# Spreading attention weights over the partitions: SBUF to SBUF transfers in place of matmuls and copies, and the last store from the ACT queue

## The chip, the cores and the metric
The kernel runs on one core of a Trainium2 chip. The core has a matrix engine (PE, with its weight loads shown as PEld), a vector engine (DVE), a scalar engine (ACT), a general engine (POOL) and a queue engine (SP); SP, ACT and POOL can issue DMA transfers. The metric is the device time of one execution in microseconds (us). The kernel before takes 203.83 us, the median of three runs (202.96 to 204.58).

## The reference
A transformer layer with a local, dilated attention and a gated MLP, 2048 tokens of width 512, in bf16. Cut to what matters:

```python
# S = 2048, D = 512, H = 32 heads of Dh = 16, W = 8 window places, dil = 2, F = 1376
q, k, v = split(layernorm(x) @ wqkv)                # each (H, S, Dh)
idx = pos[:, None] - arange(W)[None, :] * dil       # s, s-2, ..., s-14
logits = einsum("hsd,hswd->hsw", q, k[:, idx]) * Dh ** -0.5   # masked where idx < 0
attn = softmax(logits, axis=-1)                     # over the 8 window places
o = einsum("hsw,hswd->hsd", attn, v[:, idx])
h = x + o @ wo
h2 = h + (relu(layernorm(h) @ W_gate) * (layernorm(h) @ W_up)) @ W_down
```

## The kernel before
The tokens are worked in four chunks of 512 (`tk` 0 to 3). Within a chunk the steps are: layer norm, transposition of the rows (by PE, or for some chunks by a DMA transpose from SP, L472), the q, k and v projections (L524, copied out by ACT, L532), attention, the output projection (L711) with residual (L722, or L720 on ACT for chunk 0), a second layer norm, gate and up projections (L749), their product on DVE (L769), the down projection (L786), the residual (L797) and the store (L801).

Attention works in a layout in which each of the 128 partitions holds one dimension of a head and the free axis holds tokens. The channels are permuted so that a tile `t` (0 to 3) holds four of the 16 dimensions of each of the 32 heads. The parts that the change touches, with the keys the code gives the steps:

- `pr` (L571, DVE): q times shifted k for half of the window places (`hf` 0 or 1) and two tiles; an instruction of 128 x 4096, four per chunk.
- `sc` (L577, PE): sums the products over the head dimension; the score tile of one half holds 32 heads x 4 window places on its 128 partitions.
- `ex` (L593, ACT): the exponential, into an `ex` tile of 128 x 512. In chunk 0 a short mask step `mk` (L596) follows on DVE.
- `den` (L610, PE), `dl` and `dr` (L613, L616, ACT): the sum over the window and its reciprocal. In chunks 1 to 3 (`EARLY`) the weights are multiplied by the reciprocal at once (`am`, L625, DVE); in chunk 0 this is done at the end (`om`, L666).
- `bc` (L638, PE) and `be` (L644, ACT): the weights of one window place stand on 32 partitions, one for each head, but are needed on 128, four for each head. For each half, four matmuls with the 0/1 matrix `spread` (32 rows of contraction, at four row positions of PE) write four banks, and four ACT copies bring them to a tile of 128 x 8 x 512 called `ab`, eight copies per chunk.
- `mu` (L659, DVE): `ab` times shifted v, 128 x 4096, one for each tile `t`.
- `ta` (L691, POOL): in chunks 0 to 2 the first addition of the sum over the window is a DMA that accumulates one half of the `mu` result onto the other, 512 KB. Then `tr2` (128 x 1024) and `tr1` (128 x 512) on DVE (L662, L685), and in chunk 0 `om`.

The results of `pr`, of `mu` and the tile `ab` come from one pool of five tiles of 128 x 8 x 512, named `big`.

The order of the work is not left to the queues. Every step is added to a planner with an engine, an assumed length and an entry of the list `RANK`: the n-th entry is the place of the n-th added step. Each engine gets its steps in increasing order of that place, and it executes them strictly in this order; an instruction waits at the head of its engine's queue until its inputs and its buffer are ready. The planner's lengths decide which buffer a step gets and how the engines' instructions interleave in the program, not the order within one engine.

SP issues, in its order: the loads at the start, the DMA transposes and the output stores. The kernel's last chunk stores its last 128 rows in two halves (columns 0 to 255 as part 3, 256 to 511 as part 4).

Of the kernel before, what the change touches and what calls it, by code (L numbers as in the profile page):

```python
# [8 lines left out]
P = 128  # L9
BF16 = mybir.dt.bfloat16  # L10
F32 = mybir.dt.float32
I32 = mybir.dt.int32
ACT = mybir.ActivationFunctionType
# [6 lines left out]
    26, 31, 32, 17, 20, 22, 23, 25, 29, 34, 35, 28, 33, 37, 39, 41, 45, 48, 21, 27,  # L20
    30, 36, 38, 42, 44, 46, 63, 74, 40, 56, 68, 49, 51, 54, 43, 60, 72, 53, 66, 65,
    77, 70, 83, 75, 80, 90, 92, 87, 114, 102, 110, 85, 105, 93, 104, 115, 125, 129, 78, 88,
    95, 99, 103, 183, 193, 202, 132, 143, 150, 156, 152, 106, 109, 116, 123, 119, 168, 181, 216, 220,
    224, 180, 188, 217, 223, 231, 187, 196, 226, 229, 234, 162, 172, 201, 205, 207, 237, 240, 239, 245,
    247, 251, 242, 248, 243, 246, 252, 256, 259, 263, 250, 254, 265, 266, 272, 278, 269, 276, 285, 275,
    283, 273, 280, 286, 318, 322, 292, 301, 304, 314, 313, 324, 341, 311, 325, 298, 303, 334, 338, 326,
    330, 346, 354, 360, 337, 355, 317, 353, 347, 358, 370, 329, 352, 340, 348, 332, 345, 294, 350, 356,
    361, 374, 343, 365, 372, 381, 351, 362, 413, 357, 368, 367, 386, 418, 400, 425, 460, 464, 417, 427,
    457, 467, 376, 434, 446, 466, 410, 429, 437, 668, 55, 61, 52, 57, 50, 58, 47, 59, 62, 64,
    67, 84, 73, 82, 86, 71, 81, 69, 79, 89, 166, 175, 122, 136, 111, 130, 137, 190, 91, 101,  # L30
    127, 173, 149, 179, 94, 96, 163, 213, 158, 170, 98, 107, 108, 167, 208, 197, 249, 257, 244, 235,
    255, 260, 264, 268, 274, 296, 279, 302, 309, 305, 310, 307, 287, 295, 290, 293, 300, 319, 328, 364,
    369, 315, 320, 359, 363, 335, 342, 380, 382, 327, 336, 373, 375, 389, 395, 387, 392, 396, 402, 393,
    399, 398, 401, 397, 403, 405, 409, 404, 407, 411, 412, 416, 419, 420, 423, 421, 428, 422, 426, 431,
    474, 482, 441, 443, 458, 463, 453, 468, 483, 438, 448, 436, 452, 442, 451, 450, 454, 456, 488, 492,
    479, 498, 455, 487, 491, 500, 507, 461, 493, 445, 459, 481, 485, 471, 475, 496, 511, 539, 524, 533,
    520, 535, 526, 530, 541, 514, 540, 484, 502, 543, 544, 556, 581, 589, 538, 552, 559, 562, 549, 554,
    584, 587, 529, 547, 560, 564, 113, 120, 100, 124, 76, 117, 97, 112, 128, 133, 140, 144, 142, 146,
    164, 145, 154, 148, 157, 161, 209, 230, 174, 186, 198, 200, 195, 215, 182, 184, 199, 228, 189, 211,
    169, 177, 178, 194, 232, 241, 271, 281, 185, 191, 261, 253, 284, 297, 289, 282, 308, 312, 321, 331,  # L40
    339, 344, 378, 366, 377, 371, 379, 383, 385, 394, 388, 391, 390, 430, 439, 470, 490, 424, 432, 473,
    476, 440, 447, 486, 489, 406, 415, 465, 477, 501, 518, 497, 504, 508, 512, 494, 499, 521, 525, 517,
    519, 516, 522, 503, 505, 527, 528, 532, 546, 534, 537, 536, 548, 531, 542, 579, 597, 566, 594, 585,
    601, 561, 580, 609, 599, 603, 588, 592, 571, 575, 577, 600, 605, 606, 610, 595, 623, 602, 611, 582,
    614, 627, 558, 576, 574, 578, 568, 572, 565, 567, 583, 621, 648, 639, 645, 636, 649, 591, 616, 652,
    624, 635, 628, 633, 640, 655, 663, 665, 667, 632, 654, 661, 711, 650, 656, 707, 710, 644, 657, 659,
    669, 126, 138, 118, 134, 131, 139, 121, 135, 141, 147, 155, 160, 151, 171, 159, 165, 153, 176, 203,
    236, 218, 225, 192, 204, 214, 219, 258, 291, 262, 270, 222, 233, 267, 277, 227, 238, 212, 221, 288,
    316, 206, 210, 306, 299, 323, 333, 384, 349, 408, 414, 433, 435, 444, 462, 449, 506, 510, 509, 513,
    515, 469, 495, 478, 472, 480, 563, 570, 586, 593, 523, 551, 557, 569, 573, 590, 596, 598, 545, 550,  # L50
    553, 555, 615, 622, 604, 607, 612, 619, 608, 613, 626, 629, 618, 620, 630, 631, 617, 625, 634, 637,
    638, 641, 646, 653, 643, 651, 642, 647, 691, 695, 681, 692, 694, 698, 688, 697, 700, 679, 687, 674,
    677, 670, 680, 666, 671, 690, 673, 675, 672, 682, 658, 662, 660, 678, 683, 684, 689, 664, 685, 699,
    702, 676, 693, 705, 701, 706, 704, 709, 686, 703, 708, 713, 715, 716, 718, 696, 714, 719, 720, 722,
    724, 731, 712, 726, 732, 734, 717, 725, 727, 730, 728, 733, 735, 737, 721, 723, 729, 736,
]


class Op:


    __slots__ = ("eng", "dur", "lat", "fn", "deps", "prio", "take", "use", "start", "done", "seq", "key")

    def __init__(self, eng, dur, fn, deps=(), prio=0.0, take=(), use=(), lat=0.0):
        self.eng, self.dur, self.fn, self.lat = eng, dur, fn, lat
# [788 lines left out]
```

## Time and profile before
| | |
|---|---|
| median of three runs | 203.83 us (202.96 to 204.58) |
| span of the profiled execution | 200.7 us |
| PE busy | 193.4 us, 1095 instructions |
| DVE busy | 153.3 us, 239 instructions |
| ACT busy | 121.8 us, 256 instructions |
| POOL busy | 12.7 us |
| mean granted PE clock | 0.999 of full speed |
| DMA | 18.81 MB, 94 GB/s on average |

The profile is of one execution; the device time of that execution is its span and some us around it that the profile does not show (203.83 less 200.7 is 3.1 us, by the median). Times within it count from the first instruction. Matmuls are pipelined and their single durations overlap, so their step from one to the next is read from the chain of waits, not from the mean duration. A line such as L659 is the line of the kernel that issued the instruction. Idle time of an engine is followed by what ended it. In the DVE column of the page the slices from 20 to 100 us stand at 9 tenths or more almost throughout; PE stands there from the second slice to the last but one.

### The profile page before, as it was taken

To read this page: it belongs to the slowest core of one execution; us is meant where nothing else is said; L and a number is where in the kernel's file an instruction comes from. 1 tells how busy PE (TensorE), PEld (TensorE's weight loads), DVE (VectorE), ACT (ScalarE), POOL (GpSimd) and SP (SyncE) were. 2 spreads that over 40 slices of the span, in tenths; PEclk is the share of its full clock that TensorE was granted. 3 is DMA by queue.
4 is the path that set the end of the run, shared out by engine and by line. 5 is a ranking of instruction groups with operands and counts; after the bars stand their busy time and mean duration, and the time that the engine had idled before them with its cause. 6 is when DMAs were issued, how large, how long until landed. Compare 5 with 4: busy or idle time off the path is not lost.

```text
span 200.7 us, 2938 instructions
## 1 busy us (share of the span) xinstructions
PE 193.4 (96%) x1095; PEld 96.2 (48%) x1115; DVE 153.3 (76%) x239; ACT 121.8 (61%) x256; POOL 12.7 (6%) x28
## 2 busy tenths in 40 slices
PE   8999999989999999999999999999999999999992
PEld 8776445445445344444444444444444444444451
DVE  6989998989999999999996868799967412022313
ACT  3576798747899965887436779701566631277400
POOL 4000000410000013100131000000000000000000
PEclk9999999999999999999999999999999999999999
DMA  6989933994000009920399400131010050200103
GB/s 204 322 245 409 388 119 66 170 201 87 3 0 0 3 0 183 195 40 3 57 178 193 124 3 0 29 75 52 3 52 0 0 104 3 78 0 0 52 0 105
DMA packets 17676, 18.81 MB, mean 94 GB/s; under 512 B 8352, under 2 KB 14464, under 8 KB 17664
## 3 DMA queue, kind: packets, MB, share of 16 engines
q1 hardware_dynamic: 15360, 11.57, 18.5%
q0 software_dynamic: 1728, 6.29, 16.6%
q10 hardware_dynamic: 576, 0.79, 1.2%
q8 instruction: 8, 0.13, 0.3%
q14 instruction: 4, 0.03, 0.0%
HBM read 8.42 MB, written 2.10 MB: 52 GB/s over the span
## 4 chain that ended last, share of the span: by engine, by line
PE 67%; DVE 16%; DMA 6%; ACT 5%; issue 2%; SPq 1%; ACTq 0%
PE bank L749 29%; PE bank L524 15%; PE bank L786 14%; DVE big L659 6%; PE bank L711 5%; DMA quad<-row 5%; DVE big L571 3%; DVE gT L769 2%; DMA x_sm<-in_A_x_dram 1%; SPq L472 1%; PE bank L483 1%; DVE x_sm L722 1%; DVE big L662 1%; DVE row L454 1%; PE bank L577 1%
## 5 line engine op out<-in xcount | busy, mean ns | idle before, releaser
L749 PE MATMUL bank<-quad,wu_sb 128*128 128x512 bf16 (+1 forms) x172 | 42.4, 379 | 0.4
L749 PE MATMUL bank<-quad,wg_sb 128*128 128x512 bf16 (+1 forms) x173 | 42.0, 379 | 0.4 <-DMA quad<-row 0.3
L756 ACT ACTIVATE gr<-bank 128x512 bf16<-128x512 f32 (+1 forms) x44 | 25.3, 616 | 24.7 <-PE bank L749 22.9
L786 PE MATMUL bank<-wd_sb,gT 128*128 128x512 bf16 (+2 forms) x183 | 39.8, 366 | 0.2
L753 ACT CAST up_sb<-bank 128x512 bf16<-128x512 f32 (+1 forms) x44 | 25.0, 600 | 21.0 <-PE bank L749 17.3
L571 DVE TENSOR_TENSOR big<-quad,kT 128x4096 bf16<-128x4096 bf16 x16 | 36.2, 2284 | 0.2
L659 DVE TENSOR_TENSOR big<-big,vT 128x4096 bf16<-128x4096 bf16 x16 | 35.9, 2281 | 0.0
L769 DVE TENSOR_TENSOR gT<-gr,up_sb 128x1024 bf16<-128x1024 bf16 (+1 forms) x24 | 15.3, 642 | 24.0 <-ACT up_sb L753 14.4
L524 PE MATMUL bank<-quad,wqk_sb 128*128 128x512 bf16 (+1 forms) x139 | 29.9, 355 | 1.0 <-DMA quad<-row 0.8
L786 PEld LDWEIGHTS <-gT 128*128 128x128 bf16 (+1 forms) x187 | 18.1, 98 | 19.7 <-issue 0.4
L749 PEld LDWEIGHTS <-wg_sb 128*128 128x128 bf16 (+1 forms) x176 | 17.3, 100 | 21.2 <-issue 0.9
L749 PEld LDWEIGHTS <-wu_sb 128*128 128x128 bf16 (+1 forms) x176 | 17.5, 100 | 20.6 <-issue 0.7
L524 PEld LDWEIGHTS <-wqk_sb 128*128 128x128 bf16 x144 | 15.6, 114 | 12.8 <-issue 2.3
L797 DVE TENSOR_TENSOR row<-x_sm,bank 128x512 bf16<-128x512 bf16 (+1 forms) x17 | 10.6, 649 | 10.4 <-PE bank L786 10.4
L644 ACT CAST big<-bank 128x512 bf16<-128x512 f32 x32 | 17.8, 635 | 0.4 <-PE bank L638 0.2
L662 DVE TENSOR_TENSOR big<-big 128x1024 bf16<-128x1024 bf16 (+2 forms) x24 | 16.8, 728 | 0.1
L691 POOL DMA_DIRECT2D big<-big x12 | 10.5, 873 | 88.1 <-DVE big L659 59.9
L524 PE MATMUL bank<-quad,wv_sb 128*128 128x512 bf16 x62 | 15.6, 380 | 0.2
L711 PE MATMUL bank<-wo_sb,quad 128*128 128x512 bf16 x62 | 15.2, 379 | 0.2
L454 DVE TENSOR_SCALAR row<-x_sm,mv,rs 128x512 bf16<-128x512 bf16 x32 | 11.4, 407 | 3.7 <-ACT rs L436 3.1
L532 ACT CAST quad<-bank 128x512 bf16<-128x512 f32 x16 | 9.5, 612 | 4.6 <-PE bank L524 4.6
L499 ACT COPY quad<-bank 128x1024 bf16<-128x1024 bf16 (+1 forms) x9 | 8.0, 929 | 6.0 <-PE bank L483 6.0
(68 smaller groups left out, 147.2 us busy)
## 6 DMA issues: line engine op xcount, KB each, us to landing
big<-big POOLq DMA_DIRECT2D x12, 512.0 KB, 5.6
out_dram<-row SPq DMA_DIRECT2D x15, 128.0 KB, 1.8
x_sm<-in_A_x_dram SPq DMA_DIRECT2D x3, 512.0 KB, 5.5
wu_sb<-in_B_W_up_dram SPq DMA_DIRECT2D x1, 1376.0 KB, 8.6
wg_sb<-in_B_W_gate_dram SPq DMA_DIRECT2D x1, 1376.0 KB, 11.6
wd_sb<-in_B_W_down_dram SPq DMA_DIRECT2D x1, 1280.0 KB, 14.9
wqk_sb<-in_A_wqkv_dram ACTq DMA_DIRECT2D x2, 256.0 KB, 5.0
wqk_sb<-in_A_wqkv_dram SPq DMA_DIRECT2D x2, 256.0 KB, 5.2
```

What stands on the lines that cost most here:

```text
L454: V.tensor_scalar(out=xn.t[:], in0=x, scalar1=mv.t[:, j, 0:1], scalar2=rs.t[:, j:j + 1], op0=ALU.add if residual else ALU.subtract, op1=AL ...
L524: nc.tensor.matmul(mm.t[:, lo:hi], lhsT=wv_sb[:, dt, t:D:NT] if c == 2 else wqk_sb[:, dt, c * D + t:(c + 1) * D:NT], rhs=xnT.t[:, dt, lo:h ...
L571: V.tensor_tensor(out=pb.t[:].rearrange("p (t w) s -> p t w s", t=2), in0=q4, in1=k4, op=ALU.mult)
L644: nc.scalar.copy(out=ab.t[:, w, :], in_=bc.t[:])
L659: V.tensor_tensor(out=mt.t[:], in0=ab.t[:], in1=v8, op=ALU.mult)
L662: V.tensor_tensor(out=mt.t[:, 0:n, :], in0=mt.t[:, 0:n, :], in1=mt.t[:, n:2 * n, :], op=ALU.add)
L711: nc.tensor.matmul(od.t[:], lhsT=OT.t[:, t, j * P:(j + 1) * P], rhs=wo_sb[:, t, :], start=(t == 0), stop=(t == NT - 1 and tk not in RPE))
L749: nc.tensor.matmul(mm.t[:fs, :], lhsT=w_sb[:, dt, ft * P: ft * P + fs], rhs=hnT.t[:, dt, :], start=(dt == 0), stop=(dt == NT - 1))
L753: nc.scalar.copy(out=ub.t[:fs, i, :], in_=um.t[:fs, :])
L756: nc.scalar.activation(out=gr.t[:fs, i, :], in_=gm.t[:fs, :], func=ACT.Relu)
L769: V.tensor_tensor(out=gt.t[:fs, 0:n, :], in0=gr.t[:fs, 0:n, :], in1=ub.t[:fs, 0:n, :], op=ALU.mult)
L786: nc.tensor.matmul(od.t[:, c0:c1], lhsT=gts[ft].t[:fs, ft % 2, j * P:(j + 1) * P], rhs=wd_sb[:fs, ft, c0:c1], start=(ft == 0), stop=(ft == ...
```

## The change
For every chunk and half (`BCD`), the four matmuls and four ACT copies are replaced by four DMA transfers issued from SP, with the step key `bd`. Each reads the 32 partitions of one window place and writes each row to four neighbouring partitions, 128 rows of 1 KB. The tile `ab` gets a pool of its own with one tile, and the pool `big` shrinks from five to four. The store of the very last part (part 4 of chunk 3) is issued from ACT's queue. `RANK` is new throughout, with 706 entries where it had 738. The options `PRE` and `DEN1` are empty, so their branches are never taken. The planner learns of a shared DMA queue (`dq`) and has some lengths changed; these change no instruction.

```diff
-    big_s = slots(5, [P, W, CS], BF16, "big")
+    NAB = 1
+    big_s = slots(5 - NAB, [P, W, CS], BF16, "big")
+    ab_s = slots(NAB, [P, W, CS], BF16, "ab") if NAB else big_s
...
+    BCD = tuple((k, h) for k in range(4) for h in range(2))
...
-        ab, abd = Buf(big_s), []
+        ab, abd = Buf(ab_s), []
         for w0 in range(0, W, BCN):
             hf = w0 // 4
+            if (tk, hf) in BCD:
+                def f_bd(w0=w0, ab=ab, ex=exs[hf]):
+                    for w in range(w0, w0 + 4):
+                        r = w % 4 * HB
+                        nc.sync.dma_start(ab.t[:, w, :], ex.t[r:r + HB, :].unsqueeze(1).to_broadcast([HB, 4, CS]))
+
+                abd.append(add(("bd%d" % hf, tk), "SP", 4 * DMI, f_bd, [exd[hf]], apr + 1, take=[ab],
+                               use=[exs[hf]], lat=0.7, dq=(0.2, 1.54 - 3 * DMI)))
+                continue
...
+            last = tk == NCK - 1 and n == len(parts) - 1
+
+            def f_os(j=j, c0=c0, c1=c1, ob=ob, tk=tk, q=nc.scalar if last else nc.sync):
+                q.dma_start(out_rows[:, tk * BPC + j, c0:c1], ob.t[:, c0:c1])
```

Read entry by entry, the new `RANK` gives these orders (key, then chunk after the point; `xtd` and `htd` are the DMA transposes of the first and second layer norm, `hxn` the normalised rows of the second, `gu` the gate x up products, `o` the residuals of the MLP, `os` the stores). SP before, to chunk 2:

```
xtd0.3 xtd2.3 xtd1.3 xtd3.3 htd0.1 htd1.1 os0.0 os2.0 os1.0 htd1.2 htd3.2 htd0.2 htd2.2
```

SP after, to chunk 2, and its end:

```
bd1.0 bd0.0 xtd1.3 xtd3.3 xtd0.3 xtd2.3 bd1.1 bd0.1 bd0.2 bd1.2 htd1.1 htd0.1 bd0.3 os3.0 bd1.3 os1.0 os0.0 htd3.2
... os2.2 os0.3 os1.2 os0.2 os1.3 os2.3 os3.3
```

DVE before, from the second mask step of chunk 0 to the middle of chunk 1's attention (`xst`, `xag` statistics, `xxn` normalised rows of the first layer norm):

```
mk0.0 xst.3 xag.3 (4) xxn.2 (4) xxn.3 (4) mu3.0 mu0.0 mu1.0 mu2.0 pr0_2.1 tr2_3.0 tr1_3.0 om3.0 pr0_0.1 tr2_0.0 tr2_1.0
tr1_0.0 tr1_1.0 om0.0 tr2_2.0 tr1_2.0 om1.0 om2.0 ... am1.1 pr1_2.2 pr1_0.2 am0.1 pr0_2.3 pr0_0.3 mu1.1 mu0.1 mu3.1 mu2.1
gu0.0 am0.2 gu1.0 pr1_2.3 gu3.0 tr2_1.1 tr1_1.1 tr2_0.1 tr1_0.1 gu2.0 ...
```

DVE after, the same stretch and on to chunk 3's first `mu`:

```
mk0.0 xst.3 (2) xag.3 (3) xxn.2 (4) xxn.3 (3) mu3.0 xxn2.3 mu0.0 mu1.0 mu2.0 tr2_3.0 tr1_3.0 om3.0 pr0_0.1 tr2_0.0 tr1_0.0
om0.0 tr2_1.0 tr1_1.0 pr0_2.1 om1.0 tr2_2.0 tr1_2.0 om2.0 ... am1.1 hxn0.0 hxn1.0 am0.1 pr0_0.2 pr0_2.3 mu1.1 pr0_0.3 mu3.1
mu0.1 gu1.0 tr2_1.1 mu2.1 gu2.0 tr1_1.1 am0.2 pr1_0.3 am1.2 gu0.0 tr2_0.1 gu3.0 tr2_3.1 tr1_0.1 tr1_3.1 gu4.0 tr2_2.1
tr1_2.1 mu0.2 ... hxn1.1 ... mu1.2 o3.0 mu2.2 o2.0 mu3.2 am1.3 am0.3 o1.0 tr2_1.2 tr2_0.2 o0.0 tr1_0.2 tr1_1.2 tr2_2.2
gu0.1 tr1_2.2 gu1.1 tr2_3.2 tr1_3.2 mu3.3
```

PE before, from the end of chunk 0's attention to its first down projection (`htp` transposes, `ga` and `up` the gate and up projections, `dnA` the first 8 and `dnB` the last 3 column tiles of the down projection):

```
wo2.0 sc0.1 sc1.1 mm_q2.3 mm_k2.3 den.1 mm_k3.3 mm_v2.2 htp.0 (4) sc0.2 bc1.1 mm_v2.3 ga0.0 ... up9.0 dnA2.0
```

PE after:

```
wo3.0 sc1.1 mm_v3.2 mm_k1.3 den.1 mm_v2.2 mm_v1.3 sc1.2 mm_k0.3 htp.0 (4) mm_v0.3 up4.0 ... up10.0 dnA0.0
```

and its end is `... dnA2.3 dnB2.3 dnA3.3 dnB3.3`.

## The prediction
> **What bounds the kernel now.** I read the busy times first, then the windows of ten microseconds, then the chain that ended last, then the timeline around the edited lines, and last the DMA issues. Page and windows (busy time, with the number of instructions in brackets; the last three columns are the granted clock, the DMA share and GB/s):
> ```profile
> PE 193.4 (96%) x1095; PEld 96.2 (48%) x1115; DVE 153.3 (76%) x239; ACT 121.8 (61%) x256; POOL 12.7 (6%) x28
> ```
> ```profile
> 0.00:10.00 10.00, 8.51 (x91) 8.01 (x92) 7.63 (x28) 4.10 (x11) 2.20 (x16) 1.00 0.78 264
> ...
> 40.00:50.00 10.00, 9.30 (x43) 4.98 (x45) 9.36 (x12) 5.76 (x12) 0.86 (x1) 1.00 0.76 147
> ...
> 60.00:70.00 10.00, 9.85 (x82) 4.67 (x84) 10.00 (x11) 9.94 (x21) 0.00 (x0) 1.00 0.01 2
> 70.00:80.00 10.00, 9.95 (x63) 4.19 (x57) 10.00 (x5) 6.43 (x13) 2.58 (x3) 1.00 0.45 85
> ...
> 190.00:201.00 11.00, 7.10 (x43) 4.08 (x42) 3.14 (x6) 0.00 (x0) 0.00 (x0) 0.97 0.15 48
> ```
> PE is idle 7.3 us of 200.7, and 5.4 of that lie in the first and the last window. In between it is full, so the time is start + PE's own list + tail, and every us taken off PE's list counts unless a wait takes its place. Right behind PE stands DVE: full from 50 to 100 us. ACT is full only around 55 to 70.
>
> **The matmuls removed.** Lines of the chain (start, length, what):
> ```profile
> 21.70 1.85 PE bank L524 x8
> 23.55 0.33 PE bank L638 x4
> 23.88 1.85 PE bank L524 x8
> ...
> 122.83 4.32 PE bank L749 x20
> ```
> A group of four spreading matmuls holds PE 0.33 us. A normal matmul takes 4.32/20 = 0.216, so eight should take 1.73; beside a spreading group they take 1.85, so the change of form costs up to 0.12 more. Eight groups are removed: 8 x 0.33 = 2.6 to 8 x 0.45 = 3.6 us. I take 0.40 each, 3.2 us, since some groups stand next to score matmuls of the same kind. It all lies on PE's list.
>
> **The ACT copies removed.**
> ```profile
> L644 ACT CAST big<-bank 128x512 bf16<-128x512 f32 x32 | 17.8, 635 | 0.4 <-PE bank L638 0.2
> ...
> L638 PE MATMUL bank<-ex,spread 32*128 32x512 bf16 x32 | 3.2, 384 | 0.0
> ```
> In the chain one copy steps on by 0.49 us, so ACT loses 32 x 0.49 = 15.7 us. ACT is not the path, so this is worth nothing by itself; it hides under PE and DVE. What it can free is waits on ACT: DVE waits 0.47 us for the reciprocal at 44.1, 0.44 for the residual at 53.5, and 0.57 at 31 for a row buffer behind PE. Together 1.5 us of DVE's time, which matters because of what follows.
>
> **The transfers added.** Per chunk eight SyncE DMAs, each 128 rows of 1 KB, from 32 partitions. No such transfer is in the trace. The nearest rows (median us from issue to landing):
> ```profile
> big<-big POOLq DMA_DIRECT2D x12, 512.0 KB, 5.6
> out_dram<-row SPq DMA_DIRECT2D x15, 128.0 KB, 1.8
> ...
> quad<-row SPq DMA_TRANSPOSE x14, 2.5
> ```
> ```profile
> 196.06 2.29 SPq L801 DMA_DIRECT2D out_dram<-row  x5
> ```
> The row store has the same size and the same 1 KB rows: 1.8 us to land, and five issues take 2.29, so 0.46 each. Four issues for one half of the windows: 3 x 0.46 + 1.8 = 3.2 us, which I take because that row is nearest in size, form and queue. The lower end is 3 x 0.39 + 1.6 = 2.8 (the shortest of the store rows), the upper end 5.6 (512 KB in SBUF beside other traffic). The way replaced:
> ```profile
> 28.48 0.40 PE L638 MATMUL bank<-ex,spread 32*128 32x512 bf16 x4
> ...
> 28.96 0.59 ACT L644 CAST big<-bank 128x512 bf16<-128x512 f32 x1
> ...
> 29.55 1.55 ACT L644 CAST big<-bank 128x512 bf16<-128x512 f32 x3
> ...
> 31.77 8.89 DVE L659 TENSOR_TENSOR big<-big,vT 128x4096 bf16<-128x4096 bf16 x4
> ```
> From 28.48 to 31.10 is 2.6 us, so the new way has 0.2 to 3.0 us more latency. Who waits for it is the first mu multiply of a chunk, with all of DVE's list queued behind. Its cover is the DVE work that the new list has between the last ex or am step and that mu, with the steps of this trace (pr and mu 2.2, bn_stats 0.61, rows 0.34, tr2 and gate x up 0.61): chunk 0: two bn_stats, three aggregates and seven rows, 4.0 us; chunk 1: two products, 4.4 us, less 0.8 because SP is still issuing the other half; chunk 2: 4.7; chunk 3: 6.3. Against 3.2 all four are covered. Against 5.6 they are late by 1.6 + 2.0 + 0.9 + 0 = 4.5 us.
>
> [...] No run here shows a read from 32 partitions.
>
> SP's order: the chunk 0 transfers are issued near 25 and 27 us, when the weights have landed (DMA share 0.13 in 27:28, 0.00 in 28:30). The four transposes for chunk 3 stand behind them; their rows are ready at about 30 in both lists, and PE waited 0.8 us for them at 40.6, with or without the change. The transposes of chunk 1 stand behind the chunk 2 transfers, which need steps that DVE does 13 us earlier (am1 at 78.3 against hxn1 at 91.4 of its list). The store moved to ACT is the last half row by index, but the new order ends PE with dn3, whose store stays on SP. It saves one 0.46 issue ahead of that: the last DVE step ends at 197.62 and its store is issued at 197.96, so up to 0.3 us.
>
> **One buffer fewer.** Five big tiles become four plus one for the weights. Today a product runs at 40.76 between the fourth mu and the first tree step:
> ```profile
> 40.76 2.29 DVE L571 TENSOR_TENSOR big<-quad,kT 128x4096 bf16<-128x4096 bf16 x1
> 42.97 1.15 DVE L662 TENSOR_TENSOR big<-big 128x1024 bf16<-128x1024 bf16 x2
> ```
> In the new list the tree step follows mu at once, three mu = 6.6 us after the first. The accumulating DMA is issued 0.7 after its mu ends and lands 4.6 to 6.8 later, 5.3 to 7.5 in all: DVE waits 0 to 0.9. I take 0.5.
>
> **The sum.** PE's list before the first down projection holds (row steps added up) 85.2 us now and 83.2 after; the projection starts now at 87.85, 2.65 behind its list. It could start at 83.2 + 2.65 = 85.9. It needs the fourth gate x up product, which has the same 79.9 us of DVE work ahead of it in both lists and now ends at 87.51. Were DVE no faster, PE would wait 1.7 us there. DVE gets 1.5 back from the waits and loses 0.5: 1.0 earlier, 86.5, so PE waits some 0.7 (0 to 1.7). An earlier wait of 0.4 to 1.4 in front of the first up projections (the new list has one matmul group there, not three, to cover the normalised rows) is the same lateness, not another; for both I take 0.8. After 100 us DVE has idle time (8.08, 7.24 and 7.86 busy in the next three windows) and the lists leave it 1 us or more. Sum: 3.2 - 0.8 + 0.3 = 2.7 us off a profiled 200.7, that is 198.0; with 203.83 - 200.7 = 3.1 around the span, 201.1, say 201.0. The three runs spread over 1.6 us around their median.
>
> **The rivals.**
> *Forecast, 0.55:* PE keeps most of the saving, 199.9 to 201.8. For it: PE full from 10 to 197.
> *DVE paces to 87 us, 0.25:* the freed waits come back as waits for the accumulating DMAs, and PE idles 1.7 of 3.2. 203.8 - 1.5 - 0.3 = 202.0, to 203.5 if the first mu is late too. For it: DVE at 10.00 in two windows above.
> *Slower, 0.17:* the transfers land late. Place: first mu of chunks 0 to 2, where DVE has no slack. At 5.6 us a half the loss is 4.5: 201.1 + 4.5 = 205.6; at 7, with accumulating transfers on the same DMA engines, 3 x 1.4 more, 209.8. It decides from about 5.2 us a half, where the loss passes 2.7. Against it: DMA share 0.01 at 60 to 70 us, where chunk 1 needs them.
> *The store change does nothing, 0.5 inside each case:* the last store is still SP's; 0.3 us less gain.
>
> **The numbers.** A measurement of this kernel tells about 1% (2.0 us) from no change. The forecast, less a tenth of it past 201.8, and a quarter of the second give faster 0.59; most of the second and the mild part of the third, 202 to 205.8, give same 0.27; the rest of the third and what I have not seen, slower 0.14. Low end: all 3.6 + 0.3 and no wait, 199.9. High end: the second case and a third of the slower one, 204.8.
>
> **What would show it.** Spreading matmuls and copies gone, PE near 190.2 busy, ACT near 104. The eight transfers of a chunk landing 1.5 to 2.5 us after issue: right; over 4: the slower rival. DVE idle in front of the first mu of a chunk, or in front of the first tree step of chunk 0, sizes the two DVE terms. The start of the first down projection between 85.9 and 87.5 tells forecast from second case. PE idle over 3 us between 10 and 190 would make the forecast wrong.

## The result, and the profile after

| | before | after |
|---|---|---|
| median | 203.7 us (202.96 to 204.58, 4 runs) | 208.58 us (207.87 to 209.21, 4 runs) |
| ratio after to before, 95% interval | | 1.0247 [1.0204, 1.029] |
| span of the profiled execution | 200.7 us | 207.4 us (time 209.21 us) |

The change makes the kernel 2.5% slower. The forecast was 201.0 us with a range up to 204.8; the rival in which the transfers land late came true. Here and below, executions that are over 1.5% above the fastest of their kernel count in the medians but are left out of the ratios.

The page of after: busy times, and the granted clock of PE in forty slices.
```profile
PE 194.2 (94%) x1063; PEld 95.9 (46%) x1083; DVE 152.9 (74%) x239; ACT 107.5 (52%) x224; POOL 12.7 (6%) x28
...
PEclk9999999999699997999999999999999999999999
```
PE did not lose busy time, though 32 matmuls are gone. Some records are missing (1095 matmuls beside 1115 weight loads in before, 1063 beside 1083 in after), so PE's busy time can't be compared to a us. But the clock is no longer full: it falls to 0.6 and 0.7 in two slices, where before stood at 9 throughout, and PE counts as busy at a low clock too (82 to 83 us: busy 1.00 of 1.00 us at a clock of 0.50). The mean clock of 0.981 over 207.4 us is, as an estimate, 3.9 us of PE's time, which is more than the matmuls' 3.2. The clock is not the cause of the slowdown: the one execution of after with a clock of 1.000 took 207.87 us. The windows show where (busy us with instruction counts, then granted clock, DMA share, GB/s):
```profile
50.00:60.00 10.00, 7.90 (x40) 2.92 (x40) 9.90 (x11) 4.73 (x10) 0.00 (x0) 0.83 0.01 2
60.00:70.00 10.00, 9.44 (x76) 4.50 (x76) 9.59 (x13) 9.97 (x26) 0.00 (x0) 1.00 0.10 21
70.00:80.00 10.00, 7.93 (x53) 3.22 (x56) 7.79 (x5) 6.49 (x13) 0.86 (x1) 1.00 0.45 105
80.00:90.00 10.00, 9.78 (x49) 4.01 (x41) 10.00 (x9) 3.34 (x7) 2.58 (x3) 0.83 0.83 156
...
120.00:130.00 10.00, 8.79 (x41) 3.91 (x41) 5.36 (x9) 3.11 (x6) 0.00 (x0) 1.00 0.55 138
```
PE, busy for 9.30 us or more in each of before's windows from 10 to 190, has three holes: 50 to 60, 70 to 80 and 120 to 130. DVE has holes in 70 to 80 and 120 to 130 (before, 70 to 80 was 10.00), and one in 30 to 40 (7.26; before 9.41). The DMA issues point to the cause (count, KB each, median us from issue to landing):
```profile
big<-big POOLq DMA_DIRECT2D x12, 512.0 KB, 5.0
ab<-ex SPq DMA_DIRECT2D x32, 128.0 KB, 2.8
out_dram<-row SPq DMA_DIRECT2D x15, 128.0 KB, 1.8
```
A transfer lands 2.8 us after its issue, where the row store of the same size still takes 1.8. And the timeline shows what waits (start, length; in brackets the idle time before it and what ended it). Chunk 0, chunk 1, chunk 3:
```profile
26.36 6.26 SPq L674 DMA_DIRECT2D ab<-ex  x8
...
34.79 2.29 DVE L705 TENSOR_TENSOR big<-ab,vT 128x4096 bf16<-128x4096 bf16 x1 [2.74 <-DMA ab<-ex]
```
```profile
67.49 5.09 SPq L674 DMA_DIRECT2D ab<-ex  x8
...
75.05 2.29 DVE L705 TENSOR_TENSOR big<-ab,vT 128x4096 bf16<-128x4096 bf16 x1 [2.21 <-PE bank L638]
```
```profile
115.69 4.99 SPq L674 DMA_DIRECT2D ab<-ex  x4
...
121.76 2.51 SPq L674 DMA_DIRECT2D ab<-ex  x4
...
126.60 2.29 DVE L705 TENSOR_TENSOR big<-ab,vT 128x4096 bf16<-128x4096 bf16 x1 [3.49 <-DMA out_dram<-row]
```
In the three chunks the first `mu` multiply (now L705) waits 2.74, 2.21 and 3.49 us. The releasers named in the second and third row are not the cause: `mu` reads neither a PE bank nor a stored row, and its last input is the tile `ab`, whose last issues end at 72.58 and 124.27. Eight issues take 5.09 us, 0.64 each; in chunk 3, beside two accumulating transfers of POOL, the first four alone take 4.99.

Behind a late `mu` stand all of DVE's later steps, among them the next chunk's products, and PE waits for those:
```profile
PE bank L588 <- DVE big L582: 3.9, 2, 2.0
PE bank L757 <- DVE x_sm L768: 1.2, 1, 1.2
```
(Waits of PE between 27 and 195 us: total us, times, longest. All of them come to 6.4 us; before had 1.1.)

### The profile page after: what moved, and what is told of

Same layout as the page of the kernel before. It is cut to its first block, busy times and chain, and to the rows that moved or that the text cites. A ratio compares the mean times of both kernels' runs of the same rounds, so it can differ in the third digit from the quotient of the medians.

```text
span 207.4 us, 2914 instructions
## 1 busy us (share of the span) xinstructions
PE 194.2 (94%) x1063; PEld 95.9 (46%) x1083; DVE 152.9 (74%) x239; ACT 107.5 (52%) x224; POOL 12.7 (6%) x28
## 4 chain that ended last, share of the span: by engine, by line
PE 52%; DVE 27%; DMA 9%; SPq 5%; issue 5%; ACT 0%; DVEq 0%
PE bank L795 27%; PE bank L832 13%; DVE big L705 8%; DVE big L582 8%; PE bank L757 5%; DMA x_sm<-in_A_x_dram 5%; SPq L674 5%; PE bank L588 3%; DVE st L430 3%; DVE big L708 3%; DMA ab<-ex 3%; PE bank L535 2%; DVE row L465 2%; DVE x_sm L768 1%; DMA quad<-row 1%
## 5 line engine op out<-in xcount | busy, mean ns | idle before, releaser
L705 DVE TENSOR_TENSOR big<-ab,vT 128x4096 bf16<-128x4096 bf16 x16 | 36.3, 2286 | 8.8 <-DMA out_dram<-row 3.5
L802 ACT ACTIVATE gr<-bank 128x512 bf16<-128x512 f32 (+1 forms) x44 | 25.0, 602 | 30.5 <-PE bank L795 26.9
L535 PE MATMUL bank<-quad,wqk_sb 128*128 128x512 bf16 (+1 forms) x141 | 30.9, 361 | 1.0 <-DMA wqk_sb<-in_A_wqkv_dram 0.5
L795 PEld LDWEIGHTS <-wg_sb 128*128 128x128 bf16 (+1 forms) x176 | 17.8, 101 | 21.0 <-issue 1.1
L708 DVE TENSOR_TENSOR big<-big 128x1024 bf16<-128x1024 bf16 (+2 forms) x24 | 17.3, 732 | 1.3 <-DMA big<-big 1.1
L757 PE MATMUL bank<-wo_sb,quad 128*128 128x512 bf16 x63 | 15.7, 388 | 1.2 <-DVE x_sm L768 1.2
L419 ACT ACTIVATE row<-x_sm,mv 128x512 bf16<-128x512 bf16 x12 | 8.6, 718 | 12.1 <-DVE mv L411 12.1
L588 PE MATMUL bank<-big,sel 128*32 128x512 bf16 x128 | 9.2, 403 | 4.0 <-DVE big L582 3.9
L430 DVE BATCH_NORM_STATS2 st<-x_sm 128x6 f32<-128x512 bf16 x16 | 10.3, 678 | 2.5 <-DMA x_sm<-in_A_x_dram 2.5
```

What stands on the lines that cost most here:

```text
L430: V.bn_stats(out=st.t[:], in_=x_sm[:, tk * BPC + j, :])
L535: nc.tensor.matmul(mm.t[:, lo:hi], lhsT=wv_sb[:, dt, t:D:NT] if c == 2 else wqk_sb[:, dt, c * D + t:(c + 1) * D:NT], rhs=xnT.t[:, dt, lo:h ...
L588: nc.tensor.matmul(sc.t[g * HB:(g + 1) * HB, :], lhsT=sel[:], rhs=pb.t[:, 4 * u + g, :], start=(t + u == 0), stop=(t + u == NT - 1), tile_ ...
L705: V.tensor_tensor(out=mt.t[:], in0=ab.t[:], in1=v8, op=ALU.mult)
L708: V.tensor_tensor(out=mt.t[:, 0:n, :], in0=mt.t[:, 0:n, :], in1=mt.t[:, n:2 * n, :], op=ALU.add)
L757: nc.tensor.matmul(od.t[:], lhsT=OT.t[:, t, j * P:(j + 1) * P], rhs=wo_sb[:, t, :], start=(t == 0), stop=(t == NT - 1 and tk not in RPE))
```

## The experiments

**1. The parts of the change apart.** order_only keeps the order, the pools and the last store of after, and spreads by matmuls and ACT copies; the one bank more that this needs is had by spreading in groups of two. transfers_only has the transfers in the order and the pool of five tiles of before. store_only is before with the last store on ACT.
```diff
# order_only, from after; RANK: after's places, bc and be at the place of bd
-    BCD = tuple((k, h) for k in range(4) for h in range(2))
+    BCD = ()
-    BCN = 4
+    BCN = 2
# transfers_only, from after; RANK: before's places, bd at the place of bc
-    NAB = 1
+    NAB = 0
-            last = tk == NCK - 1 and n == len(parts) - 1
+            last = False
# store_only, from before
-            def f_os(j=j, c0=c0, c1=c1, ob=ob, tk=tk):
-                nc.sync.dma_start(out_rows[:, tk * BPC + j, c0:c1], ob.t[:, c0:c1])
+            def f_os(j=j, c0=c0, c1=c1, ob=ob, tk=tk, q=nc.scalar if last else nc.sync):
+                q.dma_start(out_rows[:, tk * BPC + j, c0:c1], ob.t[:, c0:c1])
```


> The changed kernel's order, buffers and last store, but the weights spread by matmuls and ACT copies as before (in groups of two matmuls, since that order leaves only three free banks). Theory (the transfers are slower than the order allows for): the first mu of each chunk no longer waits, DVE's 8.7 us of waits there go, and the time is 202 to 205.5 us. Rival (the new order and the smaller pool cost the time by themselves): 207 us or more, with DVE still idle in front of mu and of the first tree steps.

Measured: 212.43 us, ratio 1.044 [1.0377, 1.0502]. The groups of two seem to cost by themselves (PE is busy 202.03 us, against 193.4 in before with 20 records missing, and hardly waits), so this run doesn't tell what the order costs; after_none below does. DVE waits in it before chunk 1's first `mu` too (2.31 us, for ACT's copies).

> The order, the pool of five and the last store of the kernel before, with only the spreading matmuls and copies replaced by the transfers. Theory (transfers too slow for the cover): PE loses 3.2 us of work, but a half takes some 4.8 us against covers of 3.8 to 8.7, so two or three first mu wait 1 to 3 us each: 202 to 207 us. Rival (the order and pool are the cause): the saving of PE stands, 201 us or less.

Measured: 204.87 us, ratio 1.0021 [0.9982, 1.0059]. The same transfers (2.6 us to landing) in the order of before change little or nothing. In the profiled execution, one of the longer ones (205.87 us), DVE waits for them 2.33 us in chunk 0 and 1.78 in chunk 1, and not in chunks 2 and 3. So they are late here too, but in two chunks of four, and in this order the matmuls and copies saved nearly pay for it (see the stages below).

> The kernel before with only the last store moved to ACT's queue. Both theories: between 0.5 us faster and no change, since the last store waits 0.34 us for SP now. If the ACT queue lands later, up to 0.3 us slower.

Measured: 202.84 us against 203.81, ratio 0.9947 [0.9928, 0.9966]. It is faster than both kernels, by 0.5% than before. PE's last matmul ends 2.9 us before the end of the span, 3.5 us in before; this is seen in after too (2.9). It accounts for 0.6 of the 1.0; the spans (median 201.0 against 201.9) hold nearly all of it.

**2. The price of a transfer by itself.** The kernel probe is before with five groups of four transfers behind its last store, where nothing else runs.
```diff
+        for w in range(4):
+            nc.sync.dma_start(b0[:, w, :], e0[w * HB:(w + 1) * HB, :].unsqueeze(1).to_broadcast([HB, 4, CS]))
+        for w in range(4):
+            nc.sync.dma_start(b0[:, w, :], q0[:, w, :])
+        for w in range(4):
+            nc.sync.dma_start(b0[:, w, :], e0[w:P:4, :].unsqueeze(1).to_broadcast([HB, 4, CS]))
...
```


> The kernel before, and behind its last store five groups of four transfers from SP, SBUF to SBUF, with nothing else running: 32 neighbouring partitions to 128; 128 to 128; 32 partitions four apart to 128; 32 to 32; 32 to 128 with half rows. Its time is of no interest. If the price is of the transfer itself, the first group issues every 0.65 us and lands after 2.8, as in the changed kernel's median; if it came from other traffic, 0.46 and 1.8. [...]

Issue durations (ns, least, median, longest) and us to landing, for the first three groups, one line of the kernel each:
```profile
L821 SPq DMA_DIRECT2D big<-ex x4: 543/555/674, 199.3 to 201.4; - x4
...
DMA to landing us min/median/max: 2.6/2.7/2.7
```
```profile
L823 SPq DMA_DIRECT2D big<-quad x4: 465/509/665, 202.1 to 204.4; - x4
...
DMA to landing us min/median/max: 2.0/2.1/2.3
```
```profile
L825 SPq DMA_DIRECT2D big<-ex x4: 594/598/602, 205.2 to 207.1; - x4
...
DMA to landing us min/median/max: 2.1/2.1/2.1
```
The form of the kernel, 32 neighbouring partitions to 128, lands in 2.7 us with nothing beside it; 128 to 128, and 32 partitions that lie four apart, land in 2.1. The issue takes 0.5 to 0.6 in every form. So 2.7 us is the transfer's own price, not contention, and 0.6 of it belongs to reading from neighbouring partitions. Less data from the same partitions lands sooner: half rows (64 KB) in 2.1, 32 partitions to 32 (32 KB) in 1.9. A half (first issue to last landing) takes 4.7 us from neighbouring partitions and 4.0 from four apart, 0.7 more (128 to 128, whose issues came further apart, takes 4.4).

**3. Fewer transfers, or smaller ones, in chunks 1 to 3.** All are after with chunk 0 unchanged; old_order_none is transfers_only with the first edit. What isn't transferred is left out of the computation; the products read what the tile holds.
```diff
# after_none, old_order_none
-                    for w in range(w0, w0 + 4):
+                    for w in range(w0, w0 + 4 if tk == 0 else w0):
# after_two
+                    for w in range(w0, w0 + 4, 1 if tk == 0 else 2):
# after_half_rows
+                        n = CS if tk == 0 else CS // 2
+                        nc.sync.dma_start(ab.t[:, w, 0:n], ex.t[r:r + HB, 0:n].unsqueeze(1).to_broadcast([HB, 4, n]))
```


> The changed kernel with the transfers of chunks 1 to 3 left out (chunk 0's weights stay in the tile, so the output is not the layer's); order, pools, all other work as changed. Theory (the transfers' price against a cover that is too thin): DVE's waits in front of the first mu of chunks 1 and 3 (2.2 and 3.5 us) and what PE loses behind them go: 201 to 204.5 us. Rival (the new order or the smaller pool is slow by itself, as the run with the copies put back suggests): 206 us or more.

> The changed kernel with two of the four transfers of each half left out in chunks 1 to 3 (those windows keep chunk 0's weights). If SP's issues and the engines' time per transfer set the lateness, both halves land after 3 x 0.65 + 2.8 = 4.8 us instead of 7.4 and most of the wait goes: 203 to 206 us. If lateness is a fixed latency, under 0.5 us is gained.

> The changed kernel with all its transfers, but in chunks 1 to 3 of half rows (256 of 512 columns; the other columns keep chunk 0's weights): half of the bytes, all of the issues. If the issues set the pace (the probe issued half rows no faster, 0.6 us), only the last landing comes 0.6 us earlier: 206.5 to 208.5 us. If the bytes set it, as the run with two transfers of four: 203 to 206.

> The run with transfers in the old order, with those of chunks 1 to 3 left out: what taking the matmuls and copies off is worth where nothing takes their place. If PE's list is the bound as the prediction says: 203.8 less 3.2, 200 to 201.5 us. If DVE paces the kernel and PE's saving is lost anyway: 202.5 or more.

| | us | ratio to before | waits of the first `mu` in chunks 1 and 3, us |
|---|---|---|---|
| after | 208.58 | 1.0247 [1.0204, 1.029] | 2.21, 3.49 |
| after_half_rows | 204.93 | 1.006 [1.0042, 1.0078] | 1.63, 2.58 |
| after_two | 203.63 | 0.9995 [0.998, 1.0009] | 0, 1.41 |
| after_none | 203.31 | 0.9973 [0.995, 0.9995] | 0, 0 |
| old_order_none | 203.11 | 0.9962 [0.9934, 0.9991] | 0, 0 |

The transfers of chunks 1 to 3 cost 208.6 - 203.3 = 5.3 us; the new order and the smaller pool without them are no slower than before. Half as many take away 5.0 of it, half the bytes in as many transfers 3.7: the count and the bytes both matter. But without them the kernel stands only at 203.3, not at 201.

In both kernels that have transfers in chunk 0 alone, the first `mu` of that chunk is still late (2.59 us in after_none, 2.04 in old_order_none). How much of the missing 2 us this is, the stages below tell.

**4. Which queue.** after_c0_act issues chunk 0's transfers from ACT's queue, none_c0_act does so without transfers in the other chunks, and after_split issues the odd window places from ACT in all chunks.
```diff
-                        nc.sync.dma_start(ab.t[:, w, :], ex.t[r:r + HB, :].unsqueeze(1).to_broadcast([HB, 4, CS]))
# after_c0_act; none_c0_act the same on top of after_none
+                        (nc.scalar if tk == 0 else nc.sync).dma_start(ab.t[:, w, :], ex.t[r:r + HB, :].unsqueeze(1).to_broadcast([HB, 4, CS]))
# after_split
+                        (nc.scalar if w % 2 else nc.sync).dma_start(ab.t[:, w, :], ex.t[r:r + HB, :].unsqueeze(1).to_broadcast([HB, 4, CS]))
```


> As after, but chunk 0's eight transfers are issued from ACT's queue instead of SP's; chunks 1 to 3 unchanged. In after the first product of chunk 0 waits 2.74 us at 34.79 us for transfers that were issued from 26.36 us on, behind the last weight loads on SP's queue. Theory 'queued behind the weights on the same queue': on another queue they land about 2.8 us after their issue, the wait falls under 1 us, and the time falls by 1 to 2 us, to 206.6 to 207.6. Rival 'the DMA engines themselves are full of weights (share above 1.0 from 20 to 30 us)': the wait stays at 2 us or more and the time within 0.5 us of 208.6. Rival 'ACT pays': eight issues of about 0.6 us lie before the evictions that PE needs, PE gets a wait on ACT in chunk 0 and the time stays or rises.

> As after, chunk 0's transfers issued from ACT's queue, and no transfers at all in chunks 1 to 3 (their products read what the tile holds, so that part of the computation is left out). After without transfers in chunks 1 to 3 took 203.3. If the forecast's 3.2 us of PE were held back only by chunk 0's late transfers: 200.5 to 201.5. If DVE's own work in chunks 0 to 2 sets the pace: 202.8 to 203.5, with PE waiting on DVE's products (L582) as before.

> As after, but of each half's four transfers the second and the fourth are issued from ACT's queue, the others from SP's, in all chunks. Theory 'SP's pace of 0.65 us an issue, two halves behind each other on one queue, makes the lateness of chunks 1 to 3': a half's last issue comes 1.3 us earlier and the second half's up to 2.6 us earlier, the waits at mu1.1 (2.2 us) and mu3.3 (3.5 us) shrink by 1.3 us or more each and the time falls by 2 to 3.5 us, to 205 to 206.5. Rival 'the DMA engines are full, not the issuing queue': the landing after the issue grows by what the issue gains, and the time stays within 0.7 us of 208.6. Rival 'ACT pays': ACT loses 16 issues of 0.6 us = 10 us, less than the 15.7 us of copies it had before, so only its place in ACT's order could cost; then waits on ACT appear.

Measured: after_c0_act 209.74 us, ratio 1.0247 [1.0203, 1.0291], the same as after. none_c0_act 205.47, 1.0077 [1.0052, 1.0103], where after_none has 0.9973: 2 us worse. On ACT's queue the transfers of chunk 0 land no sooner (median 3.5 us in none_c0_act as in after_none), and ACT is held up by its issues, so that its next step for PE comes late:
```profile
25.99 2.90 ACTq L674 DMA_DIRECT2D ab<-ex  x4
28.94 0.60 ACT L618 ACTIVATE ex<-bank 128x512 bf16<-128x512 f32 x1 [3.12 <-PE bank L535]
...
30.36 3.02 ACTq L674 DMA_DIRECT2D ab<-ex  x3
33.43 0.21 ACT L447 ACTIVATE rs<-rs 128x4 f32<-128x4 f32 x1 [3.22 <-DMA ab<-ex]
```
The second exponential starts at 28.94 instead of 26.93. So standing behind the weights on one queue is not what makes chunk 0 late. DMA engines full of weights are not either, though the share is 1.05 in after from 20 to 30 us. In the profiled execution of after_two, whose chunk 0 is that of after, the last weight load landed at 27.7 us (29.9 in after), before the second half was issued (from 28.0 us), and the first `mu` waits as long (the DMA share is the last number but one; first after, then three lines of after_two):
```profile
27.00:28.00 1.00, 1.00 (x9) 0.57 (x6) 1.00 (x2) 0.91 (x2) 0.00 (x0) 1.00 1.10 348
```
```profile
26.00:27.00 1.00, 1.00 (x9) 0.59 (x6) 1.00 (x2) 0.88 (x2) 0.00 (x0) 1.00 0.51 119
```
```profile
25.39 6.13 SPq L674 DMA_DIRECT2D ab<-ex  x8
...
33.86 2.29 DVE L705 TENSOR_TENSOR big<-ab,vT 128x4096 bf16<-128x4096 bf16 x1 [2.78 <-DMA ab<-ex]
```
What the two share is eight transfers behind each other on one queue: their issues take 6.26 and 6.13 us, a single one of them 1.4 and 1.5. With four on each of two queues (after_split) the issues take some 4 us, none over 0.71, and the first `mu` waits 0.92 us, though there the share is 1.10 to 1.13 until 29 us. From the second exponential to the first `mu` it is 6.4 us in after_split, against 7.7 in after and after_two.

after_split 209.24 us, ratio 1.0245 [1.0186, 1.0304], the same as after. Behind chunk 0 the two queues do issue sooner (in chunk 1 the last issue starts 2.7 us after the first, in after 4.5), but the landing grows (medians over all chunks; 2.8 in after):
```profile
ab<-ex SPq DMA_DIRECT2D x16, 128.0 KB, 4.6
ab<-ex ACTq DMA_DIRECT2D x16, 128.0 KB, 4.3
```
In chunk 1 the eight transfers move at this rate, first in after, then in after_split (last three numbers: clock, DMA share, GB/s):
```profile
70.00:71.00 1.00, 0.95 (x5) 0.44 (x5) 1.00 (x2) 0.63 (x2) 0.00 (x0) 1.00 0.87 213
```
```profile
71.00:72.00 1.00, 1.00 (x6) 0.42 (x5) 1.00 (x1) 0.43 (x1) 0.00 (x0) 1.00 0.91 208
```
One queue already keeps the DMA engines 0.8 to 0.9 busy, at some 200 GB/s. SP's pace (128 KB in 0.64 us, 205 GB/s) and the engines' rate are about equal, so in this chunk to relieve the first alone is worth little: the wait is 1.99 us instead of 2.21.

That the time did not fall has a second cause, the rival 'ACT pays'. DVE's waits for `ab` before 130 us fall from 8.4 us in after to 2.9, but its waits for ACT rise from 1.8 to 7.9. The longest is in chunk 3, where ACT stands idle 4.71 us around two of its issues:
```profile
121.43 1.22 ACTq L674 DMA_DIRECT2D ab<-ex  x2
122.70 0.60 ACT L802 ACTIVATE gr<-bank 128x512 bf16<-128x512 f32 x1 [4.71 <-DMA ab<-ex]
...
123.80 0.69 DVE L815 TENSOR_TENSOR gT<-gr,up_sb 128x1024 bf16<-128x1024 bf16 x1 [4.76 <-ACT up_sb L799]
```
What a second queue is worth where its engine has nothing else to do, no run shows.

**5. Free transfers, and an order made for the measured price.** all_none has no transfers at all. retuned and retuned_b have every instruction of after, in orders that were searched with the measured durations.
```diff
# all_none
+        nc.gpsimd.memset(ab_s.tiles[0][:], 0.125)
-                    for w in range(w0, w0 + 4):
+                    for w in range(w0, w0):
# retuned, retuned_b (each with its own RANK)
-                abd.append(add(("bd%d" % hf, tk), "SP", 4 * DMI, f_bd, [exd[hf]], apr + 1, take=[ab],
-                               use=[exs[hf]], lat=0.7, dq=(0.2, 1.54 - 3 * DMI)))
+                abd.append(add(("bd%d" % hf, tk), "SP", 2.6, f_bd, [exd[hf]], apr + 1, take=[ab],
+                               use=[exs[hf]], lat=1.75, dq=(-2.0, 2.6)))
```


> As after, but with no transfers at all, in chunk 0 either: the tile ab is filled once with 0.125 by GpSimd at the start, and the products read that, so the spreading of the weights is left out of the computation. It is after's order with transfers that are free. Theory 'chunk 0's transfers, queued behind the weight loads on SP, hold back the rest of PE's saving': no wait before chunk 0's first product (2.6 us at 34.5 us in the kernel without transfers in chunks 1 to 3, which took 203.3), and 200.5 to 201.5. Rival 'DVE's own work in chunks 0 to 2 sets the pace, and PE's 3.2 us are hidden behind it': 202.7 to 203.4, with PE still idle before the scores for DVE's products (L582) between 50 and 60 us.

> As after in every instruction, but the order of the steps (RANK) was looked for anew with the transfers priced as they were measured: 0.65 us an issue, the last landing 2.15 us after the last issue began, two halves behind each other, none before the weight loads are through at 29 us. The planner in the kernel has the same prices. Theory 'the order was made for transfers that are too cheap, and that is why after is slower': the waits of DVE at mu1.1 (2.2 us) and mu3.3 (3.5 us) go under 0.7 us, and the time is 203 to 205, that is level with before. Rival 'the transfers themselves cost, wherever they stand (beside the accumulating transfers, on the DMA engines)': waits on ab of the same sum appear at other products, and the time stays above 206.5.

> A second order from the same search with the same prices as the kernel named retuned, from another start of the random choice: it shows how much of the time is the luck of one order. The two should lie within 1.5 us of each other, and both on the same side of 206 us.

all_none: 204.39 us, ratio 1.0026 [1.0003, 1.005], above both expectations. The fill disturbs the start:
```profile
0.00:10.00 10.00, 5.73 (x54) 5.56 (x55) 8.43 (x22) 2.77 (x7) 5.59 (x17) 0.94 0.77 255
10.00:20.00 10.00, 10.00 (x87) 8.24 (x85) 8.38 (x21) 5.46 (x12) 0.00 (x0) 0.89 0.90 321
```
PE has 5.73 busy us in the first window (7.41 in after_none). The time therefore doesn't answer the question, and free transfers with an undisturbed start were not measured. But from chunk 0's first `mu` on, the execution is undisturbed and can be compared; see the stages below.

retuned: 207.18 us, ratio 1.0171 [1.0121, 1.022]. retuned_b: 205.26, 1.0089 [1.006, 1.0118]. Both are faster than after, none is level with before, and they lie 1.9 us apart and on both sides of 206, more than was expected. DVE still waits before `mu` (in retuned 1.9 us in chunk 0, 1.6 in chunk 1 and 0.4 in chunk 3, in retuned_b 1.9 in chunk 0), and in retuned_b 2.1 us for an accumulating transfer. A better order wins back 1.4 to 3.3 us; how much the best one would, stays open.

## Why the prediction was wrong

The profiled spans, one execution each, are cut at two marks that every kernel has: the start of chunk 0's first `mu`, and the end of the fourth gate x up product, behind which the first down projection starts in before.

| us | before | old_order_none | after_none | all_none | after |
|---|---|---|---|---|---|
| chunk 0's second exponential starts | 26.8 | 28.0 | 26.9 | 29.4 | 27.1 |
| from there to the first `mu` | 5.0 | 6.8 | 7.6 | 4.9 | 7.7 |
| first `mu` to fourth gate x up | 55.8 | 54.9 | 55.9 | 55.9 | 59.0 |
| from there to the end of the span | 113.1 | 112.0 | 111.2 | 111.8 | 113.6 |
| span | 200.7 | 201.6 | 201.6 | 201.9 | 207.4 |

The middle stage in the windows of before, old_order_none, after_none, all_none and after (stretch and length, then busy us of PE, PE's weight loads, DVE):
```profile
31.77:87.59 55.82, 54.59 (x323) 25.80 (x328) 54.63 (x52) 44.44 (x92) 7.04 (x8) 1.00 0.45 85
```
```profile
34.74:89.60 54.86, 52.93 (x311) 24.90 (x310) 54.48 (x51) 38.33 (x81) 7.03 (x8) 1.00 0.44 84
```
```profile
34.48:90.38 55.90, 53.55 (x305) 24.42 (x304) 55.08 (x52) 37.17 (x79) 7.03 (x8) 0.97 0.44 83
```
```profile
34.26:90.13 55.87, 54.66 (x317) 25.38 (x316) 55.05 (x53) 39.74 (x83) 7.03 (x8) 1.00 0.45 85
```
```profile
34.79:93.81 59.02, 53.79 (x295) 24.22 (x300) 55.25 (x52) 36.52 (x78) 7.03 (x8) 0.94 0.52 103
```
In after's order, with late transfers before it or with none at all, this stage takes 55.9 us, of which DVE is busy 55.1. In before's order it takes 55.8 (55.8 in store_only too) and, without the matmuls and copies, 54.9; transfers_only has 56.7 with a wait of 1.78 for transfers in it, 54.9 without. PE is nearly as full as DVE in before, but in old_order_none its busy time falls by 1.7 us and the stage by 0.95 only, to 0.4 above DVE's busy time, and in after_two, at the same clock, PE is busy 52.17 us and the stage is 55.9. So DVE sets it.

**The matmuls: right in size, wrong in worth.** In before three of the eight spreading groups are issued after 88 us, and the last stage is 1.9 us shorter in after_none: 0.6 of it is the tail (the store), 1.3 is three groups of 0.43. (In all_none's execution the tail was 3.4 us, hence 111.8. In old_order_none the stage is 1.1 shorter, 0.3 of it tail, so 0.27 a group.) The prediction took 0.40 a group. The other five groups lie where DVE sets the pace and are worth nothing there by themselves. The prediction had the figures for it ("the same 79.9 us of DVE work ahead of it in both lists") and let PE wait 0.8 of its 3.2 there; it was 5 x 0.4 = 2.0.

**ACT and the waits it frees.** "DVE gets 1.5 back from the waits and loses 0.5: 1.0 earlier" came true in before's order, where DVE's 1.5 us of waits in the middle stage are gone in old_order_none and the stage is 0.95 shorter. It failed in after's order: the waits fall to 0.4 in after_none, but DVE's busy time between the marks rises by 0.45, since other short steps lie there, and the stage is no shorter. ACT lost 14.3 us of busy time (121.8 to 107.5; predicted 15.7), and nothing else of it can be seen in the time. So the rival "DVE paces to 87 us" was right about the stage in after's order. With transfers that are always in time the kernel would gain the last stage's 1.9 us: 203.8 - 1.9 = 201.9, the 202.0 of that rival. In before's order, without the store, it would be 0.95 + 1.1: 201.8. Both are worked out, not measured.

**The transfers: the step that decided.** "Four issues for one half of the windows: 3 x 0.46 + 1.8 = 3.2 us, which I take because that row is nearest in size, form and queue." The issue's pace is 0.64 and the landing 2.8: 3 x 0.64 + 2.8 = 4.7 us for one half alone (4.7 in the probe too, with nothing beside it), so the cover was too thin in chunks 0 and 1 even then. The row store was not a near row: in the probe a read from 32 neighbouring partitions lands 0.6 us later than one from 128 (2.7 against 2.1), and 128 to 128 within SBUF still 0.3 later than the store (1.8). And halves are seldom alone: "Against 3.2 all four are covered" let a half stand behind the other half's issues for 0.8 us in chunk 1 and for nothing elsewhere. From the end of the last input to the start of `mu` it took in after:

- chunk 0: the mask ends at 28.39, `mu` starts at 34.79: 6.4 us, against a cover of 3.7 (DVE's work to 32.06; 4.0 predicted), late by 2.7. The eight issues took 6.26 us, where eight of 0.46 would take 3.7. The prediction also had "the weights have landed (DMA share 0.13 in 27:28)", read from one execution. In that microsecond the share is 1.10 in after and 1.12 in store_only: the last weight load was issued at 15.29 and 14.45 us, in before at 13.65, since the loads ahead of it wait for POOL's copy on chunk 1's rows of `x` (SP waits 5.9 us for it in after, 4.9 in before), and these came later: the loads start at 11.03 us in after and store_only, at 9.39 in before. But after_two, where the weights landed earlier, is late by as much (2.78), so this is not what made chunk 0 late.
- chunk 1: the second `am` ends at 68.45, `mu` starts at 75.05: 6.6 us against the cover of 4.4 that the prediction had worked out, late by 2.2. The second half's issues stand behind the first half's.
- chunk 2: covered, as predicted.
- chunk 3: the second `am` ends at 115.67, `mu` starts at 126.60: 10.9 us, late by 3.5, where the prediction had 6.3 of cover. Two accumulating transfers ran at the same time (DMA share 0.97 to 1.07 in each microsecond from 114 to 120); single issues took up to 1.87 us and landings up to 6.4.

The table shows what this cost. Chunk 0's lateness is the 2.7 us more before the first `mu`. Chunk 1's 2.2 and a wait of 0.7 for ACT behind it make up 2.9 of the 3.2 us more of the middle stage, as DVE sets it. Chunk 3's 3.5, in a stage where DVE has idle time, cost 113.6 - 111.2 = 2.4. Together 2.7 + 3.2 + 2.4 - 1.9 = 6.4 of the 6.7 us between the spans; the rest is the 0.3 by which the second exponential was later.

The range of 2.8 to 5.6 us was too low at its upper end; the rival's other price, 7 us beside accumulating transfers, was the near one, and its point of decision, 5.2 us a half, was passed in three chunks. Its 209.8 is 1.2 above the time measured, which is partly luck: it put the late transfers in chunks 0 to 2, they came in 0, 1 and 3, and it kept a gain of 2.7 us of which 1.9 came. The prediction's sign against itself, PE idle over 3 us between 10 and 190, showed: it is 7.9 us.

**One buffer fewer.** The wait before chunk 0's first tree step, set at 0.5, did not come; one of 1.1 us for an accumulating transfer came before chunk 2's last tree step (121.96).

**The store.** Priced at 0.3 us, with none as a rival; measured alone it is 1.0. One issue fewer ahead of the last one shows as the 0.6 of the tail; where the other 0.4 is, no run tells.

**The base.** "With 203.83 - 200.7 = 3.1 around the span": after spends 1.8 us around its span in each run, and the runs of before a median of 1.85. The profiled execution of before was a short one; the median span of its other runs is 201.9. This is 1.3 us and doesn't change the sign.

## What to carry to other kernels

Price a new transfer by a row with the same source and the same number of partitions, or try it behind the end of the kernel first: here the nearest row by size was 0.9 us short in landing and 0.2 in each issue. Count all the transfers that stand behind each other on its queue, and ask what else is on the DMA engines at that place; for times near the start, look at more than one execution. And before an engine's shorter list is counted, cut the span at the marks where another engine hands over: a saving counts only in the stages that this engine sets (in after_none three of the eight groups gave 1.3 us, the other five nothing).

## What the runs showed of the hardware

After PE waits of 1.88 and 2.02 us the granted clock fell to 0.50 for some us (after_none; after, at 52.8 and 79.6). In after_none (the wait, then windows of one microsecond; the clock is the third number from the end):
```profile
52.53 0.62 PE L588 MATMUL bank<-big,sel 128*32 128x512 bf16 x8 [1.88 <-DVE big L582]
```
```profile
53.00:54.00 1.00, 1.00 (x7) 0.41 (x4) 0.93 (x3) 0.81 (x2) 0.00 (x0) 0.68 0.09 16
54.00:55.00 1.00, 1.00 (x4) 0.32 (x3) 1.00 (x2) 1.00 (x3) 0.00 (x0) 0.50 0.00 0
55.00:56.00 1.00, 1.00 (x4) 0.44 (x3) 1.00 (x1) 0.24 (x1) 0.00 (x0) 0.50 0.00 0
56.00:57.00 1.00, 1.00 (x5) 0.34 (x3) 1.00 (x2) 0.02 (x1) 0.00 (x0) 0.61 0.00 0
57.00:58.00 1.00, 1.00 (x6) 0.44 (x5) 1.00 (x1) 0.67 (x2) 0.00 (x0) 1.00 0.00 0
```
PE counts as busy all that time; only the clock and the matmuls in a window, four instead of six, show that it is slow. By the clocks this is 0.32 + 0.50 + 0.50 + 0.39 = 1.7 us of PE's time. It doesn't come each time: after_two has a wait of 1.9 us at the same place and no slice of its clock below 9. After 1.2 us (after, at 129.56) the clock stayed at 1.00. At the end it costs little where DVE sets the pace: after_none takes 203.3 us in the mean of six executions with a mean clock of 0.999 or 1.000, and 203.4 in four with 0.992. Among the four of after it may be more: 207.87 at 1.000, 209.21 at 0.981.

An SBUF to SBUF transfer took 0.5 to 0.6 us to issue in the probe, in each of the five forms; among eight on one queue in chunk 0 single ones took 1.3 to 1.7, and beside two accumulating transfers in chunk 3 up to 1.87. In the probe one of 128 KB landed in 2.7 us from 32 neighbouring partitions, and in 2.1 from 32 that are four apart or from 128. In chunk 1 eight of them moved at some 200 GB/s, from one queue or from two; the median landing rose from 2.7 to 4.2 us with two.

The start differs between executions with the same loads: the first step on chunk 1's rows of `x` begins at 9.16 us in before and at 10.80 in store_only.
